# Packed attention and top-1 expert layer: two slots of 256 rows, not four, ahead of the last phase

## The chip, the core and the metric

One core of a Trainium2 chip runs the whole program. The metric is the time of one execution on the device in microseconds (us), the median of several executions; smaller is better. Engines: PE (matrix products), PEld (its weight loads, which overlap PE), DVE (vector), ACT (scalar), POOL (GpSimd, which here mostly issues indirect DMAs), SP (SyncE, which here issues direct DMAs).

## What is computed

```python
# q, k, v: (8 batches, 8 heads, 576 rows, 64); p: (8, 8, 32, 64)
p_packed = softmax(p @ k.T / 8) @ v                  # 32 packed rows per head
x = softmax(q @ p_packed.T / 8) @ p_packed           # laid out as (4608, 512)
logits = x @ w_gate + modality_bias[modality_id]     # 8 experts
e = argmax(logits, 1); gate = softmax(logits)[n, e[n]]
out[n] = gate[n] * (relu(x[n] @ w1[e[n]]) @ w2[e[n]])   # 512 -> 1024 -> 512
```

Each row of the 4608 goes through one expert. Everything is float32; a product is made of three products of the parts of a number, the high part (fp32r) and the residual: high x high, high x residual, residual x high.

With the inputs of the timing, expert 4 gets 2311 rows, expert 5 gets 1406, expert 7 gets 891, the others none. (These counts follow from the reference on the given inputs.)

## The kernel before, in words

Attention runs over batches. Two batches are a pair (there are four pairs), and when a pair's rows of x have been written to a scratch array in device memory (`x_scr`), `routing` finds each row's expert and its place in that expert's list, and puts nine indirect DMAs for the pair into a list `pending`: `scatter` (L488) writes the rows' numbers and gates into the lists (`lst`).

The expert layer works in slots: a slot is a number of rows of one expert that are taken through both products together. There are three phases of slots.

- Phase a (slots 0 and 1): 256 rows each, from pairs 0 and 1 alone, so that they can start while the attention of the later pairs runs.
- Phase b (slots 2 to 5): 256 rows each, from pairs 0 to 2 alone, so that no row of the last pair is waited for. They must be full slots.
- Phase c (the rest): up to 512 rows each, of all pairs; the first of an expert is cut to 384 rows where that avoids an empty fourth tile of 128 (column 6 of the phase's table says which). With these inputs there are seven: 384 and 512 rows of expert 4; 384, 512, 512 of expert 5; 384, 512 of expert 7.

The expert and the rows of each slot stand in tables (`tab_a`, `tab_b`, `tab_c`) that DVE works out at run time, so the slot code loads its values from them and branches on flags. A change of expert means that weights are loaded by SP (L720 for w1, L724 for w2) and split into high part and residual. At the start of phase b and of phase c, the weights of the expert that follows are loaded ahead.

For slot n the steps are these. `go_on(n)` (L1165 and on) issues the last scatter-out of the slot before (L898), empties `pending` as far as slot n+1 needs, calls `turn_of(n+1)` (16 DVE transposes that turn the gathered rows of slot n+1, L802), and puts the loads of slot n+2 into `pending`: one load of list rows into `mt` (L761), then for each tile of 128 rows two indirect gathers `xt<-x_scr,mt` (L768), four in a slot of 256 rows and six in one of 384. `slot(n)` then does the first product (L826 for 256 rows, with four DVE steps L832 that make the residual of the hidden rows; L845 for more rows), prepares the turned rows of slot n+1 (L808, L809) and does the second product (L881). In phases a and b `feed` hands one entry of `pending` to POOL after a step of ACT, so that the entries are spread over the slot.

The numbers of slots are set here, and the end of `pending` here:

```python
    NA = (NP // 2, NP - 1)                                            # (2, 3) pairs
    SA = [max(0, -((E * (P2 - 1) - m * 2 * S) // P2)) for m in NA]    # [2, 6]
...
        if n < SA[1]:
            if n >= SA[0]:
                turn_of(n + 1)
            pre(n + 2)
            if n + 1 == SA[1]:
                held.append(pending.pop())
            if n + 2 >= SA[1]:
                flush()
```

`SA[1]` is the first slot of phase c. `flush()` without an argument hands POOL all that is left in `pending`, the scatters of the last pair among it, because the list rows of a slot of phase c may lie among them.

In the attention part the order of PE, DVE, ACT and SP is written out by hand; POOL, and every engine behind the attention, is ordered by a scheduler when the kernel is built.

Of the kernel before, what the change touches and what calls it, by code (L numbers as in the profile page):

```python
# [23 lines left out]
def packed_attn_moe_kernel(  # L24
# [113 lines left out]

    NA = (NP // 2, NP - 1)
    SA = [max(0, -((E * (P2 - 1) - m * 2 * S) // P2)) for m in NA]  # L140
    NB0 = -(-(N - SA[1] * P2) // P4)
    NB1 = (N - SA[1] * P2 + E * (P4 - 1)) // P4
    NS_ = SA[1] + NB1

# [65 lines left out]
    def need(n):  # L210
        return NA[0] if n < SA[0] else NA[1] if n < SA[1] else NP

# [449 lines left out]
    def two_slots():  # L662


        g = nc.gpsimd
        n = SA[0]
        cnt = sm.tile([P, E], F32, name="cnt_a", bufs=1)
# [130 lines left out]
    def turn(n, ts):  # L798
        g, x = (z[:, ts].rearrange("p t (j n) -> p (t j) n", n=P) for z in (xt_of(n), W["xt"][n >= SA[1]]))
        for z in range(0, P, Q):  # L800
            for w in range(0, P, Q):
                nc.vector.transpose(out=x[w:w + Q, :, z:z + Q], in_=g[z:z + Q, :, w:w + Q])  # L802
# [117 lines left out]
    def xt_of(n):  # L920
        return xts[n % 2 if n < 3 else 1 if n < SA[1] else 2]
# [231 lines left out]
    def last_out(n):  # L1153
        if n >= SA[1]:
            st_out(W, mts[n % 4], 0)

    def go_on(n):
        last_out(n - 1)
        sw(n, 1)
        flush(n + 1)  # L1160
# [8 lines that stand above are left out]
        slot(n)  # L1169
        run(n + 1)  # L1170

    def run(n):
        if n == NS_:
            last_out(n - 1)
        elif n < SA[1] + NB0:
            go_on(n)
# [41 lines left out]
```

## Time and profile before

| | |
|---|---|
| median of 3 runs | 591.72 us (591.26 to 593.12) |
| profiled execution, its own time | 589.05 us |
| its span on the core | 587.5 us |
| PE busy | 549.9 us, 94% |
| DVE busy | 337.6 us, 57% |
| POOL busy | 209.6 us, 36% |
| ACT busy | 208.7 us, 36% |
| mean granted clock of PE | 0.962 of full |

The span runs from the first to the last instruction of the core; the profiled execution's time is 1.55 us longer, and the median of the timed runs is 2.67 us above the profiled one. PE has work for nearly the whole span; the other engines are idle for about half of it or more. All times below count from the start of the span.

### The profile page before, as it was taken

To read this page: it belongs to the slowest core of one execution; us is meant where nothing else is said; L and a number is where in the kernel's file an instruction comes from. 1 tells how busy PE (TensorE), PEld (TensorE's weight loads), DVE (VectorE), ACT (ScalarE), POOL (GpSimd) and SP (SyncE) were. 2 spreads that over 40 slices of the span, in tenths; PEclk is the share of its full clock that TensorE was granted. 3 is DMA by queue.
4 is the path that set the end of the run, shared out by engine and by line. 5 is a ranking of instruction groups with operands and counts; after the bars stand their busy time and mean duration, and the time that the engine had idled before them with its cause. 6 is when DMAs were issued, how large, how long until landed. Compare 5 with 4: busy or idle time off the path is not lost. (4 is left out here: it accounts for less than half of the span.)

```text
span 587.5 us, 11603 instructions
## 1 busy us (share of the span) xinstructions
PE 549.9 (94%) x4408; PEld 461.4 (79%) x4408; DVE 337.6 (57%) x756; ACT 208.7 (36%) x371; POOL 209.6 (36%) x257
## 2 busy tenths in 40 slices
PE   5999997796999999999999999999999999999990
PEld 4777775564788898998999888898888888988880
DVE  1389995758887746453774827349356256285300
ACT  2588884446441212222211324322221242322210
POOL 4003005833355336444443242383503314904120
PEclk9899998967799999999999999999999999999996
DMA  9799996937234742117622124543201202312311
GB/s 290 243 347 370 402 335 221 246 101 244 76 112 114 179 156 70 40 39 162 223 93 65 42 69 107 128 116 122 92 1 56 73 20 58 51 38 62 30 39 39
DMA packets 33685, 77.39 MB, mean 132 GB/s; under 512 B 6768, under 2 KB 6944, under 8 KB 32576
## 3 DMA queue, kind: packets, MB, share of 16 engines
q1 hardware_dynamic: 24224, 54.92, 28.9%
q0 software_dynamic: 8848, 21.28, 13.4%
q8 instruction: 44, 0.72, 0.5%
q14 instruction: 41, 0.34, 0.2%
q10 hardware_dynamic: 528, 0.13, 0.1%
HBM read 57.04 MB, written 19.28 MB: 130 GB/s over the span
## 5 line engine op out<-in xcount | busy, mean ns | idle before, releaser
L768 POOL DMA_INDIRECT xt<-x_scr,mt x86 | 85.6, 995 | 92.1 <-issue 21.8
L802 DVE STREAM_TRANSPOSE rawv<-xt 32x384 f32<-32x384 f32 (+1 forms) x192 | 92.3, 481 | 14.4 <-DMA xt<-x_scr,mt 10.6
L881 PE MATMUL ps_o<-rawq,rawk 128*128 128x512 f32 x272 | 87.2, 391 | 0.0
L898 POOL DMA_INDIRECT out_dram<-ot,mt x37 | 37.3, 1008 | 135.8 <-ACT ot L887 110.5
L845 PE MATMUL ps_h<-x_wide,w1h 128*128 128x512 f32 (+1 forms) x168 | 62.3, 371 | 0.0
L845 PE MATMUL ps_h<-x_wide,w1l 128*128 128x512 f32 (+1 forms) x168 | 61.9, 368 | 0.0
L845 PE MATMUL ps_h<-pT,w1h 128*128 128x512 f32 (+1 forms) x168 | 61.3, 365 | 0.0
L826 PE MATMUL ps_h<-x_hl,w1h 128*128 128x256 f32 x320 | 58.1, 283 | 1.2 <-issue 0.9
L881 PEld LDWEIGHTS ps_o<-rawq,rawk 128*128 128x128 f32 x272 | 51.0, 188 | 10.4
L488 POOL DMA_INDIRECT lst<-meta,dsi x36 | 36.6, 1016 | 52.9 <-ACT st L346 32.5
L826 PEld LDWEIGHTS ps_h<-x_hl,w1h 128*128 128x128 f32 x320 | 49.9, 189 | 2.0 <-issue 1.2
L850 DVE SCALAR_TENSOR_TENSOR rawk<-ps_h,rawk 128x512 fp32r<-128x512 f32 (+1 forms) x28 | 17.4, 633 | 56.9 <-ACT rawk L849 41.2
L826 PE MATMUL ps_h<-x_hl,w1l 128*128 128x256 f32 x160 | 45.4, 285 | 0.0
L887 ACT ACTIVATE ot<-ps_o,mt 128x512 f32<-128x512 f32 x24 | 16.5, 688 | 70.0 <-PE ps_o L881 41.2
L881 PE MATMUL ps_o<-qT,rawk 128*128 128x512 f32 x96 | 37.5, 391 | 0.0
L845 PEld LDWEIGHTS ps_h<-pT,w1h 128*128 128x128 f32 x168 | 31.6, 188 | 4.1
L845 PEld LDWEIGHTS ps_h<-x_wide,w1l 128*128 128x128 f32 x168 | 31.4, 187 | 4.2
L845 PEld LDWEIGHTS ps_h<-x_wide,w1h 128*128 128x128 f32 x168 | 31.6, 188 | 4.0
L300 PE MATMUL ps<-rawv,a1T 64*64 64x128 f32 x576 | 26.9, 299 | 8.3 <-issue 6.5
L849 ACT ACTIVATE rawk<-ps_h 128x512 fp32r<-128x512 f32 (+1 forms) x28 | 15.2, 552 | 49.4 <-PE ps_h L845 47.3
L300 PEld LDWEIGHTS ps<-rawv,a1T 64*64 64x64 f32 x576 | 20.4, 147 | 14.8 <-issue 11.4
L826 PEld LDWEIGHTS ps_h<-x_hl,w1l 128*128 128x128 f32 x160 | 30.2, 189 | 0.1
(266 smaller groups left out, 1138.9 us busy)
## 6 DMA issues: line engine op xcount, KB each, us to landing
rawq<-in_q_dram SPq DMA_DIRECT2D x8, 1152.0 KB
rawv<-in_v_dram SPq DMA_DIRECT2D x8, 1152.0 KB
x_scr<-xs SPq DMA_DIRECT2D x8, 1152.0 KB
raw<-in_moe_w_dram SPq DMA_DIRECT2D x32, 256.0 KB
rawk<-in_k_dram SPq DMA_DIRECT2D x7, 1152.0 KB
kT<-in_moe_w_dram SPq DMA_DIRECT2D x4, 1024.0 KB
qT<-in_moe_w_dram SPq DMA_DIRECT2D x3, 1024.0 KB
xt<-x_scr,mt POOLq DMA_INDIRECT x86
```

Of the source, the lines that this page charges most:

```text
L300: nc.tensor.matmul(pp[u][os_, 0:P], a1T[rs, c, os_], v_t[rs, 2 * pr:2 * pr + 2, TOK[c], :], start=(c == 0), stop=(c == NC - 1), skip_group ...
L488: ins = ins_of(nc.gpsimd.indirect_dma_start(out=lst, out_offset=bass.IndirectOffsetOnAxis(ap=dsi[:, c:c + 1], axis=0), in_=meta[:, i * NC ...
L768: return [free(nc.gpsimd.indirect_dma_start(out=xt[:, t - 2 if t > 1 else 3 - t, u * HW:u * HW + HW], out_offset=None, in_=x_scr[0:NA[ph] ...
L802: nc.vector.transpose(out=x[w:w + Q, :, z:z + Q], in_=g[z:z + Q, :, w:w + Q])
L826: nc.tensor.matmul(ps[:, f], M[a][:, j, (f0 + f) * P:(f0 + f) * P + P], M["x"][b][:, j, 0:P2], start=(n == 0), stop=(n == 3 * KD - 1))
L845: nc.tensor.matmul(ps, M[a][:, j, f * P:f * P + P], M["x"][b][:, j, cs], start=(n == 0), stop=(n == 3 * KD - 1))
L849: ia = nc.scalar.activation(out=hh, in_=ps, func=AF.Relu)
L850: iv = nc.vector.scalar_tensor_tensor(out=hl, in0=ps, scalar=0.0, in1=hh.bitcast(F32), op0=ALU.max, op1=ALU.subtract)
L881: nc.tensor.matmul(op, hid(M, a, j, 1, slice(t * P, t * P + P))[:, 0], M[b][j // 4][:, j % 4], start=(n == 0), stop=(n == 3 * KF - 1))
L887: ia = nc.scalar.activation(out=ot, in_=op, func=AF.Copy, scale=mt.bitcast(F32)[:, row_of(t), 2:3])
L898: nc.gpsimd.indirect_dma_start(out=out, out_offset=bass.IndirectOffsetOnAxis(ap=mt[:, row_of(t), 1:2], axis=0), in_=M["ot"][t == 0], in_of ...
```

## The change

One line limits phase b to two slots more than phase a, so that `SA` is [2, 4] and not [2, 6]:

```diff
@@ -138,6 +138,7 @@
 
     NA = (NP // 2, NP - 1)
     SA = [max(0, -((E * (P2 - 1) - m * 2 * S) // P2)) for m in NA]
+    SA[1] = min(SA[1], SA[0] + 2)
     NB0 = -(-(N - SA[1] * P2) // P4)
     NB1 = (N - SA[1] * P2 + E * (P4 - 1)) // P4
     NS_ = SA[1] + NB1
```

With these inputs phase b then takes slots 2 and 3 (expert 4, as before), and phase c has eight slots: 384, 512, 512 rows of expert 4, and the same five of experts 5 and 7 as before. In all there are 12 slots and not 13: two of 256 rows less, one of 512 rows more. The changes of expert stay two. Lines from 141 on have a number one higher in the changed kernel.

Two places in the order of the built program matter below.

POOL, during slot 1, before: from the first gather of slot 3's rows (into `xt_142`) to the last. `lst<-meta` is a scatter of the last pair, `out_dram<-ot` writes finished rows.

```order
L761 DMA mt_139<-lst 128x2x4 [waits Activation_49]
L768 DMA xt_142<-x_scr,mt_139 128x256 [waits DMASW0_49,Activation_49]
L768 DMA xt_142<-x_scr,mt_139 128x256 [waits Activation_49]
L768 DMA xt_142<-x_scr,mt_139 128x256 [waits DMASW3_49,Activation_49]
L488 DMA lst<-meta,dsi 40960x4 [waits DMASW4_49,DVE_49,Activation_49]
L898 DMA out_dram<-ot,mt_137 4608x512 [waits DMASW5_49,Activation_49]
L768 DMA xt_142<-x_scr,mt_139 128x256 [waits DMASW6_49]
```

The same stretch of POOL after the change:

```order
L769 DMA xt_142<-x_scr,mt_139 128x256 [waits DMASW0_49,Activation_49]
L489 DMA lst<-meta,dsi 40960x4 [waits DVE_49]
L769 DMA xt_142<-x_scr,mt_139 128x256 [waits DMASW3_49,Activation_49]
L489 DMA lst<-meta,dsi 40960x4 [waits DMASW4_49]
L489 DMA lst<-meta,dsi 40960x4 [waits DMASW5_49]
L489 DMA lst<-meta,dsi 40960x4 [waits DMASW6_49]
L489 DMA lst<-meta,dsi 40960x4 [waits DMASW7_49]
L489 DMA lst<-meta,dsi 40960x4
L769 DMA xt_142<-x_scr,mt_139 128x256 [waits DMASW1_49,Activation_49]
L489 DMA lst<-meta,dsi 40960x4 [waits DMASW2_49,Activation_49]
L899 DMA out_dram<-ot,mt_137 4608x512 [waits DMASW3_49,Activation_49]
L769 DMA xt_142<-x_scr,mt_139 128x256 [waits DMASW4_49]
```

The last of the four gathers stood 5 places behind the first, and now stands 11 behind it: seven scatters lie between them where one did, since the emptying of `pending` comes at slot 2 and not at slot 4. The next slot's list load and its six gathers follow this stretch, with two more scatters and one write of finished rows ahead of the gathers.

DVE, in slot 3, before: the turn of slot 4's rows, the four residuals of slot 3's hidden rows (L832), and slot 4's residuals (L809).

```order
L802 STREAM_TRANSPOSE xt_141<-xt_142 32x8x32 x16
L659 TENSOR_LOAD tab_b
L1068 COMPARE_AND_BRANCH
L743 TENSOR_TENSOR qT<-kT,rawq 128x1024 x2
L1056 UNCONDITIONAL_BRANCH
L1068 UNCONDITIONAL_BRANCH
L832 SCALAR_TENSOR_TENSOR rawk<-ps_h_2886,rawk 128x512
L774 UNCONDITIONAL_BRANCH
L832 SCALAR_TENSOR_TENSOR rawk<-ps_h_2887,rawk 128x512
L832 SCALAR_TENSOR_TENSOR rawk<-ps_h_2888,rawk 128x512
L832 SCALAR_TENSOR_TENSOR rawk<-ps_h_2889,rawk 128x512
L809 TENSOR_TENSOR x_hl<-xt_141,x_hl 128x4x128 x2
```

The same place after the change:

```order
L803 STREAM_TRANSPOSE rawv<-xt_2876 32x12x32 x16
L660 TENSOR_LOAD tab_b
L1069 COMPARE_AND_BRANCH
L744 TENSOR_TENSOR qT<-kT,rawq 128x1024 x2
L1057 UNCONDITIONAL_BRANCH
L1069 UNCONDITIONAL_BRANCH
L833 SCALAR_TENSOR_TENSOR rawk<-ps_h_2886,rawk 128x512
L833 SCALAR_TENSOR_TENSOR rawk<-ps_h_2887,rawk 128x512
L833 SCALAR_TENSOR_TENSOR rawk<-ps_h_2888,rawk 128x512
L833 SCALAR_TENSOR_TENSOR rawk<-ps_h_2889,rawk 128x512
```

The turn ahead of slot 3's residuals is now that of a slot with three tiles, 16 transposes of 384 columns and not of 256. Before the change this longer turn stood in slot 5.

## Rows read from the trace of the kernel before

**Rows 1.** The page: the span, and PE's busy time and instructions.

```profile
span 587.5 us, 11603 instructions
...
PE 549.9 (94%) x4408; PEld 461.4 (79%) x4408; DVE 337.6 (57%) x756; ACT 208.7 (36%) x371; POOL 209.6 (36%) x257
```

**Rows 2.** PE's waits, 184.3 to 575: what for, total, times, longest.

```profile
PE ps_h L826 <- issue: 0.9, 2, 0.4
PE ps_h L826 <- ACTq L1068: 0.4, 1, 0.4
```

**Rows 3.** PE's timeline, first matmuls of slots 4, 5, 7, 8.

```profile
254.00 0.41 PE L826 MATMUL ps_h<-x_hl,w1h 128*128 128x256 f32 x2
...
276.45 0.41 PE L826 MATMUL ps_h<-x_hl,w1h 128*128 128x256 f32 x2
...
332.13 0.40 PE L845 MATMUL ps_h<-x_wide,w1h 128*128 128x512 f32 x1
...
375.92 0.35 PE L845 MATMUL ps_h<-x_wide,w1h 128*128 128x384 f32 x1
```

**Rows 4.** POOL's timeline, 199 to 210: start, duration, [idle before it, releaser].

```profile
200.66 0.99 POOL L768 DMA_INDIRECT xt<-x_scr,mt  x1 [8.61 <-DMA mt<-lst]
...
204.45 0.99 POOL L488 DMA_INDIRECT lst<-meta,dsi  x1 [0.30 <-ACT ot L887]
...
207.07 0.99 POOL L768 DMA_INDIRECT xt<-x_scr,mt  x1 [0.30 <-issue]
```

**Rows 5.** POOL's timeline, gathers of slots 4 and 6, and slot 6's list load.

```profile
226.38 0.94 POOL L768 DMA_INDIRECT xt<-x_scr,mt  x1 [0.30 <-issue]
...
260.39 0.79 POOL L761 DMA_DIRECT2D mt<-lst  x1 [0.22 <-issue]
263.58 1.02 POOL L768 DMA_INDIRECT xt<-x_scr,mt  x1 [2.40 <-DMA lst<-meta,dsi]
...
270.02 0.95 POOL L768 DMA_INDIRECT xt<-x_scr,mt  x1 [0.30 <-issue]
```

**Rows 6.** DVE's timeline, turns of slots 3, 4 and 6 and the steps behind.

```profile
214.31 7.17 DVE L802 STREAM_TRANSPOSE xt<-xt 32x256 f32<-32x256 f32 x16 [0.45 <-DVEq L1068]
221.52 1.89 DVE L832 SCALAR_TENSOR_TENSOR rawk<-ps_h,rawk 128x512 fp32r<-128x512 f32 x3
223.32 1.28 DVE L809 TENSOR_TENSOR x_hl<-xt,x_hl 128x512 fp32r<-128x512 f32 x2
229.27 7.18 DVE L802 STREAM_TRANSPOSE xt<-xt 32x256 f32<-32x256 f32 x16 [4.66 <-DMA xt<-x_scr,mt]
236.59 0.69 DVE L832 SCALAR_TENSOR_TENSOR rawk<-ps_h,rawk 128x512 fp32r<-128x512 f32 x1
...
275.82 9.32 DVE L802 STREAM_TRANSPOSE rawv<-xt 32x384 f32<-32x384 f32 x16 [7.57 <-DMA xt<-x_scr,mt]
```

**Rows 7.** PE's timeline, the second products of slot 2 and slot 3.

```profile
220.62 0.40 PE L881 MATMUL ps_o<-rawq,rawk 128*128 128x512 f32 x1
...
224.29 0.62 PE L881 MATMUL ps_o<-rawq,rawk 128*128 128x512 f32 x2
...
243.55 0.62 PE L881 MATMUL ps_o<-rawq,rawk 128*128 128x512 f32 x2
```

**Rows 8.** Slot 3's list load (POOL), w1 loads of phases b and c (SP).

```profile
191.28 0.78 POOL L761 DMA_DIRECT2D mt<-lst  x1
...
184.43 6.70 SPq L720 DMA_DIRECT2D raw<-in_moe_w_dram  x8
...
268.44 7.31 SPq L720 DMA_DIRECT2D raw<-in_moe_w_dram  x8
```

**Rows 9.** Windows: stretch, length, busy PE, PEld, DVE, ACT, POOL, clock, DMA, GB/s.

```profile
133.10:136.50 3.40, 0.50 (x17) 0.25 (x9) 3.23 (x7) 3.40 (x7) 0.00 (x0) 1.00 1.01 355
136.50:143.30 6.80, 5.78 (x66) 4.91 (x69) 6.45 (x16) 5.74 (x9) 3.93 (x4) 0.50 0.70 261
...
180.90:184.30 3.40, 2.80 (x15) 1.92 (x13) 3.02 (x13) 0.69 (x1) 1.56 (x2) 1.00 0.02 1
```

## The prediction

> **What bounds the kernel now.** I first read the page's busy times: PE has 549.9 us of work in a span of 587.5 [rows 1], far more than any other engine. Then PE's waits behind the attention: from 184.3 to 575 it idles 1.3 us in all, in three waits of 0.4 us or so [rows 2]. So in the stretch that the change touches PE alone sets the time, and a microsecond of matmuls there is a microsecond of the end. Third came PE's timeline at the slots' borders, for what a slot costs [rows 3], and last the timelines of POOL and DVE in slots 1 to 6, for how early each slot's rows are ready before PE asks for them [rows 4 to 8]. The reader is to see two things: PE has no slack, and the feeders (list load, gathers, turn) have some, but only a little of it in slot 2.
>
> **PE's work.** The change takes out two slots of 256 rows and adds one of 512 of the same expert. A slot of 256 takes 276.45 − 254.00 = 22.45 us, one of 512 takes 375.92 − 332.13 = 43.79 [rows 3]. The sum is 43.79 − 2 × 22.45 = **−1.1 us**. Nearly all of it is in the first product: 192 matmuls of 256 columns become 96 of 512, and the second product has 96 matmuls of 512 either way. The number of weight changes stays, and so do their loads and splits. Per pair of matmuls the rows give about 1.1 / 96 = 12 ns.
>
> The Trainium skill (TensorE: Matmul & The Clock Gate, "Wait — 56ns, not 53.3ns?") has a fixed cost per matmul at the full clock, about 2.5 ns on top of the columns. By it 96 matmuls less would save an estimated 0.24 us and not 1.1, and the sum below would come out 0.9 us higher. The rows here show the larger saving, since a slot of either kind was measured whole, and I go by them.
>
> **The rows of slot 3, in slot 2.** This is where the change costs something. With two slots in phase b, the emptying of the whole list of pending DMAs comes at slot 2, so seven scatters of the last pair stand among slot 3's gathers on POOL where one did. POOL issues its indirect DMAs one by one: before, the first of slot 3's gathers starts at 200.66 and the last, five places on, at 207.07 [rows 4], so a place costs 6.41 / 5 = 1.28 us. Eleven places on, the last starts at 200.66 + 11 × 1.28 = 214.8, which is 7.7 us later. The nearest landing is that of slot 4's last gather, issued at 226.38, when the turn that waits for it starts at 229.27 [rows 5, 6]: 2.89 us. So slot 3's turn starts at 214.8 + 2.9 = 217.7 and not at 214.31 [rows 6], 3.3 us later. Of the 7.7 us some 4.4 were slack.
>
> What is queued behind it: the turn keeps DVE for 7.2 us, and the residuals of slot 2's hidden rows (second to fourth of L832) stand behind it, then slot 3's residuals (L809). Before, the second residual runs from 221.52 and takes about 0.69 [rows 6]. The second product of slot 2 starts at 220.62, and its 17th matmul, at 224.29, is the first that needs that residual [rows 7] (sixteen that don't are set ahead of it; each takes 0.23 us). Before, it is ready at 222.2, so 2.1 us early. After, it is ready at 221.5 + 3.3 + 0.7 = 225.5, against 224.29: PE waits **1.25 us**. The third and fourth residuals follow 0.6 us apart and are needed later than that, and L809 ends about 3.3 us after the 224.6 of before, 227.9, still ahead of slot 3's first matmul.
>
> The bounds: by the shortest pitch in the rows (0.94 + 0.30 = 1.24 [rows 5]) the turn starts 0.45 us earlier and the wait is 0.8. The longest landing in these rows is that of slot 6's last gather, 270.02 to 275.82, 5.8 us [rows 5, 6], issued beside a weight load [rows 8]; with it the wait would be 4.2. At the time in question no weight load of that size should run, so I take the short landing, but keep 0.8 to 4.2.
>
> **The rows of slot 4, in slot 3.** Slot 4 is now the first wide one. Its list load comes behind the stretch above, at about 216, and its first gather, with two scatters and a write ahead of it, at 221 to 223: behind the list load by 3.2 us at least, as for slot 6 (260.39 to 263.58 [rows 5]). Six gathers take 6.4 us from first to last (263.58 to 270.02), so the last is issued at 227.5 to 229.5 and has landed between 230.4 (by 2.9) and 235.3 (by 5.8). The turn of three tiles takes 9.32 us, not 7.2 [rows 6]. It stands ahead of all four residuals of slot 3, and the first of these is needed by the third matmul of slot 3's second product, at 243.55 [rows 7] plus the 1.25 of the first wait, 244.8. The first residual is ready 0.85 us behind the turn's end, as before (229.27 + 7.18 to 236.59 + 0.69 is 0.83), so at 240.5 to 245.5. I take **0**, since all but the last 0.7 us of this interval is in time; the far end is 0.7.
>
> **What is later.** From slot 4 on, each slot does what slots 6 to 12 did, at the same distances from the turn to the slot: slot 6's turn ends at 275.82 + 9.32 = 285.1 [rows 6], some 14 us before that slot starts, which is at 276.45 + 22.45 = 298.9 [rows 3]. Fewer slots and tables save some steps on DVE, ACT and POOL, which hide under PE and are worth 0.
>
> **Sum.** −1.1 + 1.25 + 0 = about +0.15 us. On the profiled execution's 589.05 that is 589.2; its span is 587.5 and the median of the timed runs is 591.72, 2.67 above it. I add the difference to the median: **591.9 us**. A measurement of this kernel can tell about 0.3%, 1.8 us, from no change, so this forecast is "no change".
>
> **The rivals.**
> - *No wait at all.* The gathers' pitch or the landing come out short enough, or the slack in slot 2 is larger than read. Against it: even the shortest pitch leaves 0.8 us. PE's −1.1 stands alone: 590.6, still within 0.3%.
> - *The wait lowers PE's clock.* In the attention, a PE that had been idle for most of 3.4 us (0.50 busy) at the full clock ran the next 6.8 us at half of it, 1.2 and not 2.4 GHz [rows 9]. Another gap, of 0.6 us in 3.4 (2.80 busy), left the clock full [rows 9]. A wait of 1.25 us is nearer to the second. If the clock falls for 3.4 to 6.8 us, PE loses half of that, 1.7 to 3.4 us: 593.6 to 595.3. This is the one that ends on the slower side, and the wait of 4.2 us among the bounds would resemble the first gap more than the second. It decides as soon as the clock is lost for 3.4 us, since 1.25 − 1.1 + 1.7 = 1.85 is over 0.3%.
> - *Slot 4's rows come late.* The load of w1 ahead of phase c is issued by SP when L809 of its slot is done, which after the change is slot 2's, at about 228, just when slot 4's gathers land. In slot 1 something of the kind is seen: the load of slot 3's list rows, issued at 191.28 behind a w1 load of eight DMAs from 184.43 [rows 8], is waited for until 200.66, with POOL idle for 8.6 us [rows 4]. If slot 4's last gather needed as long (9.4 us), it would land at 237 to 239, the first residual be ready at 247 to 249, and PE wait 2.3 to 4.2 us more: 594.2 to 596. Against it: gathers issued ahead of the load, or just as it starts, need not wait behind it, and slot 6's, issued in the middle of one [rows 8], took 5.8.
> - *The change does nothing*, since the planner would have chosen the same slots: excluded, the built order has them.
>
> On the third: the Trainium skill (DMA: Bandwidth & Descriptors, "SWDGE vs HWDGE vs iDMA") says that each DMA engine goes round between the queues that software and hardware feed. By that a gather beside a weight load would be slowed, not held until the load is through, and the rival would give nothing like 9.4 us. The list load of slot 3 took that long all the same, so the trace does not bear the rule out for a small transfer; I give the rival a chance for it.
>
> **Chances.** A wait of about 1.25 us that gives back the saving: 0.50. No wait or nearly none: 0.15. The clock falls: 0.15. Slot 4's rows late: 0.12. The remaining 0.08 is for what I haven't seen, mostly longer. The first two are within 0.3%, save where the timed median drifts down: faster 0.07, same 0.63, slower 0.30. The range goes from 590.2 (no wait, and 0.4 us for the median's own scatter) to 595.3 (the clock at half for 6.8 us), which leaves out the worse half of the late rows and half of the rest on each side.
>
> **What would show it.** Right: slots 2 and 3 begin at the same times as before, POOL's last gather of slot 3 starts at about 214.8, the turn at 217.7, PE idles 1 to 1.5 us at the 17th matmul of slot 2's second product, and every slot from 4 on runs without a gap. Wrong: no gap there; or a granted clock of 0.5 near 225; or a second gap near 244, with DVE waiting for a DMA ahead of the wide turn; or slots of 512 rows of another length than 43.8 us.

## The result and the profile after

The changed kernel takes 599.88 us (median of 6 runs, 595.14 to 608.76), the kernel before 591.49 (6 runs, 589.59 to 593.12). The ratio is 1.0115, its interval 1.0069 to 1.0162: slower by 1.2%, where "no change" was forecast, and outside the range that was given (590.2 to 595.3). The profiled execution took 599.59. (Two of the changed kernel's runs, 605.65 and 608.76, are left out of the ratio, being over 1.5% above its fastest; the experiments come back to that spread.)

The page, to be read against [rows 1]: the span is 10.5 us longer, and PE's busy time is not.

```profile
span 598.0 us, 11382 instructions
...
PE 547.8 (92%) x4312; PEld 456.0 (76%) x4312; DVE 338.1 (57%) x756; ACT 208.6 (35%) x371; POOL 207.4 (35%) x256
```

So PE idles more, and the chain of waits of PE from 184.3 to 590 (what for, total, times, longest) says for what, against [rows 2]:

```profile
PE ps_h L827 <- issue: 6.5, 8, 1.7
PE ps_o L882 <- issue: 1.1, 2, 0.8
PE ps L463 <- DVE inc L458: 0.3, 1, 0.3
```

The wait that was forecast, of the second product (L882) for DVE, is not there; the one wait for DVE belongs to the routing (L463). "Issue" means that no semaphore, DMA or engine that the trace shows held PE: its next instruction simply came late. PE's timeline shows where, from 208 on, the starts of the first and second products of slots 2 and 3, and of slot 4:

```profile
210.38 0.77 PE L827 MATMUL ps_h<-x_hl,w1h 128*128 128x256 f32 x5
...
212.55 0.28 PE L827 MATMUL ps_h<-x_hl,w1h 128*128 128x256 f32 x1
213.97 0.36 PE L827 MATMUL ps_h<-x_hl,w1h 128*128 128x256 f32 x1 [1.15 <-issue]
216.08 0.37 PE L827 MATMUL ps_h<-x_hl,w1l 128*128 128x256 f32 x1 [1.74 <-issue]
216.82 0.37 PE L827 MATMUL ps_h<-x_hl,w1h 128*128 128x256 f32 x1 [0.37 <-issue]
218.25 0.37 PE L827 MATMUL ps_h<-x_hl,w1h 128*128 128x256 f32 x1 [1.06 <-issue]
218.97 0.58 PE L827 MATMUL ps_h<-x_hl,w1l 128*128 128x256 f32 x1 [0.34 <-issue]
220.39 0.60 PE L827 MATMUL ps_h<-x_hl,w1h 128*128 128x256 f32 x2 [0.85 <-issue]
...
231.10 0.39 PE L882 MATMUL ps_o<-rawq,rawk 128*128 128x512 f32 x1
...
242.02 0.41 PE L827 MATMUL ps_h<-x_hl,w1h 128*128 128x256 f32 x2
...
253.54 0.40 PE L882 MATMUL ps_o<-rawq,rawk 128*128 128x512 f32 x1
...
265.90 0.35 PE L846 MATMUL ps_h<-x_wide,w1h 128*128 128x384 f32 x1
```

From 212.6 to 220.4 the starts lie 0.72 us apart or a multiple of it (216.08 to 216.82, 218.25 to 218.97), where these matmuls otherwise follow each other in 0.12 us. I call this **the stretch**. The first product of slot 2 takes 231.10 − 210.38 = 20.72 us; that of slot 3, undisturbed, 253.54 − 242.02 = 11.52, and before the change that of slot 2 took 11.5 as well (209.09 to 220.62 [rows 7]):

```profile
209.09 0.41 PE L826 MATMUL ps_h<-x_hl,w1h 128*128 128x256 f32 x2
```

What POOL does in the same time, its timeline from 201 (the rows left out are DMAs of the same length, each 0.30 or 0.31 us behind the one before):

```profile
201.76 0.99 POOL L769 DMA_INDIRECT xt<-x_scr,mt  x1 [8.24 <-DMA mt<-lst]
203.05 0.99 POOL L489 DMA_INDIRECT lst<-meta,dsi  x1 [0.30 <-DVE red L520]
...
215.85 0.99 POOL L769 DMA_INDIRECT xt<-x_scr,mt  x1 [0.30 <-issue]
216.83 0.83 POOL L762 DMA_DIRECT2D mt<-lst  x1
217.97 0.99 POOL L489 DMA_INDIRECT lst<-meta,dsi  x1 [0.30 <-issue]
```

The stretch begins 11 us behind the start of the first of these DMAs and ends 2.4 us behind the start of the last. Windows of 3.4 us over it (busy PE, PEld, DVE, ACT, POOL, granted clock, DMA share, GB/s):

```profile
208.20:211.60 3.40, 3.40 (x22) 3.00 (x21) 0.00 (x0) 0.00 (x0) 2.79 (x3) 1.00 0.75 278
211.60:215.00 3.40, 1.59 (x12) 1.39 (x11) 0.00 (x0) 0.00 (x0) 2.49 (x4) 1.00 0.35 28
215.00:218.40 3.40, 0.90 (x3) 0.58 (x2) 0.00 (x0) 0.00 (x0) 2.79 (x4) 0.51 0.45 127
218.40:221.90 3.50, 2.31 (x10) 2.06 (x10) 0.03 (x1) 1.28 (x2) 0.96 (x2) 0.50 0.06 6
221.90:225.30 3.40, 3.40 (x18) 3.40 (x18) 3.30 (x8) 0.00 (x0) 1.56 (x2) 0.50 0.22 78
225.30:228.70 3.40, 3.40 (x30) 3.40 (x30) 3.30 (x8) 0.73 (x2) 2.72 (x3) 1.00 0.25 67
```

Behind the first starved window the granted clock falls to half, 1.2 GHz, and stays there until 225.3, some 5 us longer than the stretch. DVE and ACT do next to nothing in the stretch: they wait for PE, and the DMA engines are far from full.

The span's 10.5 us are then: slot 2 begins 1.29 us later (in the profiles of the result and of `a_again`, `a_second` and `a_third` below its start lies between 207.7 and 210.4, so two executions differ by as much), its first product is 9.2 longer (5.5 of it the waits shown, the rest the half clock and the slow steps between), slot 3's second product 1.43 longer (two more issue waits, 1.1 us, beside a run of seven DMAs), PE's work 1.12 shorter, the remainder −0.3.

The wait that was forecast is covered. DVE's timeline in slot 2:

```profile
221.87 0.69 DVE L833 SCALAR_TENSOR_TENSOR rawk<-ps_h,rawk 128x512 fp32r<-128x512 f32 x1 [14.43 <-ACTq L1069]
222.48 7.19 DVE L803 STREAM_TRANSPOSE xt<-xt 32x256 f32<-32x256 f32 x16
229.70 1.29 DVE L833 SCALAR_TENSOR_TENSOR rawk<-ps_h,rawk 128x512 fp32r<-128x512 f32 x2
```

The turn waits for no DMA: it stands behind a residual that PE's slow product delivers late, and the rest are ready before the second product asks.

### The profile page after: what moved, and what is told of

It reads as the page before. It is cut to its first block, busy times and chain, and to the rows that moved or that the text cites. A ratio compares the mean times of both kernels' runs of the same rounds, so it can differ in the third digit from the quotient of the medians.

```text
span 598.0 us, 11382 instructions
## 1 busy us (share of the span) xinstructions
PE 547.8 (92%) x4312; PEld 456.0 (76%) x4312; DVE 338.1 (57%) x756; ACT 208.6 (35%) x371; POOL 207.4 (35%) x256
## 5 line engine op out<-in xcount | busy, mean ns | idle before, releaser
L803 DVE STREAM_TRANSPOSE rawv<-xt 32x384 f32<-32x384 f32 (+1 forms) x224 | 106.3, 474 | 5.5 <-DVEq L1069 1.2
L882 PE MATMUL ps_o<-rawq,rawk 128*128 128x512 f32 x224 | 72.7, 391 | 0.3 <-issue 0.3
L846 PE MATMUL ps_h<-x_wide,w1h 128*128 128x512 f32 (+1 forms) x192 | 71.8, 374 | 0.0
L846 PE MATMUL ps_h<-x_wide,w1l 128*128 128x512 f32 (+1 forms) x192 | 71.2, 371 | 0.0
L846 PE MATMUL ps_h<-pT,w1h 128*128 128x512 f32 (+1 forms) x192 | 70.6, 368 | 0.0
L882 PEld LDWEIGHTS ps_o<-rawq,rawk 128*128 128x128 f32 x224 | 42.0, 188 | 9.5 <-issue 1.0
L827 PE MATMUL ps_h<-x_hl,w1h 128*128 128x256 f32 x192 | 37.8, 294 | 4.1 <-issue 4.0
L827 PEld LDWEIGHTS ps_h<-x_hl,w1h 128*128 128x128 f32 x192 | 32.2, 201 | 5.1 <-issue 4.6
L301 PEld LDWEIGHTS ps<-rawv,a1T 64*64 64x64 f32 x576 | 20.5, 139 | 19.5 <-issue 15.2
L882 PE MATMUL ps_o<-qT,rawk 128*128 128x512 f32 x88 | 34.3, 390 | 0.8 <-issue 0.8
L882 PE MATMUL ps_t<-rawq,rawk 128*128 128x512 f32 x104 | 34.1, 389 | 0.0
L827 PE MATMUL ps_h<-x_hl,w1l 128*128 128x256 f32 x96 | 28.6, 299 | 2.5 <-issue 2.5
```

The costliest lines, as they stand in the source:

```text
L301: nc.tensor.matmul(pp[u][os_, 0:P], a1T[rs, c, os_], v_t[rs, 2 * pr:2 * pr + 2, TOK[c], :], start=(c == 0), stop=(c == NC - 1), skip_group ...
L827: nc.tensor.matmul(ps[:, f], M[a][:, j, (f0 + f) * P:(f0 + f) * P + P], M["x"][b][:, j, 0:P2], start=(n == 0), stop=(n == 3 * KD - 1))
L846: nc.tensor.matmul(ps, M[a][:, j, f * P:f * P + P], M["x"][b][:, j, cs], start=(n == 0), stop=(n == 3 * KD - 1))
L882: nc.tensor.matmul(op, hid(M, a, j, 1, slice(t * P, t * P + P))[:, 0], M[b][j // 4][:, j % 4], start=(n == 0), stop=(n == 3 * KF - 1))
```

## Experiments

Theories. **Run**: an unbroken run of POOL's indirect DMAs, whatever they move, slows PE's issuing, and the clock falls behind that. **Scatters**: it is these seven scatters, or their targets. **Place**: it is slot 2 (its code, the weights being loaded then), or the two-slot phase as such. **Wait**: as forecast, the last gather's lateness alone, which PE pays for in the second product.

The jobs fell into two groups: in one the kernel before takes 587 to 593 us, in the other 571 to 578. Below they are the *590* and the *575* jobs; each ratio is against the kernel before in the same job. The expectations speak of two kinds of chip. The record has a chip number for each job, and number 6 stands by a job of either group (the kernel before at 575.04 us, and 13 minutes later at 590.12), so that it is the chip which differs is not shown.

### The changed kernel again

`a_again`, `a_second`, `a_third` (590 jobs) and `a_fourth` (575) are the changed kernel as it is.

> The changed kernel once more, to see whether its lost time is always in the same place. In the profile after, slot 2's first product took 20.8 us where 11.5 are normal: PE issued its matmuls 0.72 us apart from 212.6 to 220.4 with nothing named as the reason, and its clock was at half from 215.0 to 225.3. Theory 1 (the run of scatters that stands among slot 3's gathers holds PE's instructions back): the same stretch again, slot 2's first product 16 to 21 us, some 600 us. Rival 2 (such stretches come by chance and anywhere): slot 2's first product is 11.5 us here, or the stretch is in another slot, and the time is near 591 in some executions.

> The changed kernel again, since the last three kernels ran on a chip where the kernel before takes 575 us and not 589 to 592, and where no profile shows PE's slow issuing, not even in the attention. If the slow stretch in slot 2 needs a chip on which PE's issuing is slow in the attention too (L300 with waits that nothing is named for), then: on a chip of 575 us no stretch, slot 2's first product 11.5 us, a wait of 1 to 3 us in its second product, and -1 to +3 us against before; on a chip of 589 us or so again 7 us more. If the stretch comes from the program alone, slot 2's first product is 16 to 21 us on either.

> The changed kernel once more beside these. On a chip with slow issuing as before, 19 to 21 us for slot 2's first product. On one without it: the forecast of the prediction for slot 2, first product 11.5 us, a wait of 1 to 2 us at the 17th matmul of its second product, and a time within 0.3% of before.

> The changed kernel once more, for a chip on which the kernel before takes 574 to 575 us and shows no slow issuing. There: slot 2's first product 11.5 us, a wait of 1 to 2 us at the 17th matmul of its second product, slot 4's rows late by up to 3 us in slot 3's second product, and -1 to +6 us against before as the clock holds or falls. On a chip of 590 us: as in the runs before, 594 to 605.

In the 590 jobs: 596.57 (ratio 1.010, 1.0028 to 1.0172), 604.91 (596.81 to 610.33, no interval), 599.34 (1.0131, 1.0054 to 1.0208). The stretch is in all three profiles, and the first product of slot 2 takes 19.9, 20.0 and 28.7 us. In the last of them, an execution of 605.22, POOL's run did not break: DMAs from 201.51 to 228.87 with 0.3 us between them, where in the first profile it broke behind 217.97. Its stretch lasts from 213 to 231, and PE's issue waits in first products behind the attention (L827) sum to 12.4 us against 6.5. The changed kernel's spread of 594 to 611 us may come from this, whether POOL's run breaks behind that list load; with one profile of the long kind it is not shown.

In the 575 job the kernel takes 579.8 against 575.73, ratio 1.0075 (1.005 to 1.01). There the first product of slot 2 is whole (195.01 to 206.54, 11.53 us) beside the same run of DMAs, and the forecast wait is there. PE:

```profile
214.79 0.73 PE L882 MATMUL ps_o<-rawq,rawk 128*128 128x512 f32 x2 [4.42 <-DVE rawk L833]
```

POOL, the first and the last gather of slot 3:

```profile
189.54 0.99 POOL L769 DMA_INDIRECT xt<-x_scr,mt  x1 [9.96 <-DMA mt<-lst]
...
203.63 0.99 POOL L769 DMA_INDIRECT xt<-x_scr,mt  x1 [0.30 <-issue]
```

DVE:

```profile
206.81 7.20 DVE L803 STREAM_TRANSPOSE xt<-xt 32x256 f32<-32x256 f32 x16 [7.04 <-DMA mt<-lst]
214.04 1.89 DVE L833 SCALAR_TENSOR_TENSOR rawk<-ps_h,rawk 128x512 fp32r<-128x512 f32 x3
```

And the clock, by windows:

```profile
212.20:215.60 3.40, 0.81 (x4) 0.68 (x5) 3.32 (x8) 1.14 (x2) 2.79 (x3) 1.00 0.38 113
215.60:219.00 3.40, 3.40 (x10) 2.63 (x9) 1.53 (x3) 0.00 (x0) 2.26 (x3) 0.51 0.31 88
```

The last gather starts 14.09 us behind the first, as forecast (11 × 1.28 = 14.08), the turn 3.18 us behind it (forecast 2.89), and PE waits at the 17th matmul. The wait is 4.42 and not 1.25, since here the first gather leads the start of slot 2 by 5.47 us (195.01 − 189.54), 2.96 less than in the trace of before (209.09 − 200.66 = 8.43). Slot 1 is 1.06 us shorter than before (23.68 against 24.74), slot 3's list load is issued 0.53 later in it, and POOL's first gather comes 10.75 us behind that issue, not 9.38. 1.25 + 2.96 + 0.29 is 4.5. Then 3.4 us of half clock: the second product takes 17.25 us instead of 10.92, 6.3 more, of which 1.1 come back in the wide slot, so 5.2 by this profile; the timed medians differ by 4.1.

### One part of the change alone

`b_burst` is the kernel before (four slots in phase b) with only the last pair's scatters handed over at slot 2, as the change does (`flush_lists`, whose own lines are left out here, hands POOL every scatter in `pending`):

```diff
+            elif n == SA[0]:
+                flush_lists()
```

`a_lists_first` is the changed kernel with these scatters ahead of slot 3's gathers:

```diff
             pre(n + 2)
+            if n == SA[0] - 1:
+                feed()
+                flush_lists()
```

`a_three` is the changed kernel with three slots in phase b:

```diff
-    SA[1] = min(SA[1], SA[0] + 2)
+    SA[1] = min(SA[1], SA[0] + 3)
```

> The kernel before with its thirteen slots, but with all nine scatters of the last pair handed to POOL at slot 2 and not spread over slots 2 to 5: of the change only the early emptying of the list. Theory 1 (the run of scatters): PE's slow stretch and the half clock appear in slot 2's first product, which takes 16 to 21 us, and the time is 597 to 602. Rival (the stretch belongs to the new sequence of slots, or comes from the wide slot's list load and gathers): no stretch in slot 2, 591 to 593 with at most the 1.25 us wait in slot 2's second product that I forecast.

> The changed kernel, with the nine scatters of the last pair moved ahead of slot 3's gathers, behind slot 3's list load, where POOL stood idle for 8.2 us. If it is the place of the run beside the weight load of w2 and slot 2 (theory 1 in its narrow form), the stretch in slot 2 goes and the time is 589.5 to 591.5, below the kernel before by the 1.1 us of PE's work. If any run of scatters does it, the stretch moves into slot 1 and the time stays at 596 to 602. If the scatters have nothing to do with it, slot 2 is as slow as in the profile after.

> Phase b with three slots (slots 2 to 4), so that the list is emptied one slot later, with three scatters in a row and not five. PE's own work: with five slots of 256 rows the seven wide ones of before stay, so one slot of 256 less than before may be full only by its rows; the matmuls lie between those of before and after. Theory 1: no slow stretch in slot 2, 590 to 593. If the number of slots in phase b matters by itself: between before and after, 594 to 597.

All in 590 jobs. `b_burst`: 601.35, ratio 1.0225 (1.0161 to 1.0289), and again 603.4, 1.0256 (1.0213 to 1.03), as `b_burst_second`; the stretch is in slot 2's first product, 211 to 218, with waits as long as this one:

```profile
213.81 0.37 PE L831 MATMUL ps_h<-x_hl,w1h 128*128 128x256 f32 x1 [1.73 <-issue]
```

So it is not the two-slot phase: the order of POOL's work does it alone, and without the 1.1 us that the change saves. (Its profile has a second loss as well, a wait of 2.3 us in slot 4's second product, whose residuals stand behind two turns on DVE.)

> The kernel before with the early emptying alone, on the same chip as the others of this call. On a chip with slow issuing in the attention: 12 us above before, as in its first run. On one without: no stretch, and a wait of PE in slot 2's second product, 3 to 5 us above before as the last gather of slot 3 starts some 7 us later than in before.

`a_lists_first`: 603.42, 1.0247 (1.0191 to 1.0302). It puts the scatters where POOL waited for slot 3's list load anyway, so that slot 3's rows have nothing new ahead of them, and yet it is slower than the changed kernel: POOL's run lies at 183.92 to 203.07 now, and the stretch has gone with it, to 191 to 207, into the first product of slot 1, which takes 27.4 us where before took 12.9. PE's issue waits behind the attention are 13.5 us in 15. `a_three`: 595.42, 1.0101 (1.0067 to 1.0135). Its run is at 228.25 to 245.99, mostly gathers, with no weight load beside it, and the stretch at 240 to 249.5, in slot 3; its slot 2 has two issue waits of 0.3 us. Place falls: the stretch goes where the run goes.

### Other work for POOL

Each is the kernel before with work added that nothing uses: in slot 2, seven gathers (`b_gathers`, the diff) or in their place seven copies of a tile of rows (`b_work`); among the wide slots, ten gathers (`b_wide`), which stand in the code of slot 8 and which POOL issues during slot 6, not slot 7 as the expectation has it.

```diff
             pre(n + 2)
+            if n == SA[0]:
+                for j in range(7):
+                    nc.gpsimd.indirect_dma_start(
+                        out=xts[2][:, j % 4, j // 4 * HW:j // 4 * HW + HW], out_offset=None, in_=x_scr[0:NA[1] * 4 * S],
+                        in_offset=bass.IndirectOffsetOnAxis(ap=mts[3][:, 2, 0:1], axis=0))
```

> The kernel before with seven gathers added on POOL among slot 3's gathers, in the place of the scatters that the change brings there; they read rows of x that are never used, and the scatters stay spread over slots 2 to 5. Theory 1a (any unbroken run of a dozen indirect DMAs on POOL slows PE's instructions): a slow stretch in slot 2's first product, which takes 16 to 21 us, and the time 5 to 10 us above the kernel before. Theory 1b (it is the scatters, with their 16-byte rows): slot 2's first product 11.5 us, and at most some 7 us of wait in its second product behind the later turn of slot 3's rows.

> The kernel before with seven copies of 128 x 512 on POOL among slot 3's gathers, some 1.3 us each and no DMA; what they write is never used. Rival (it is POOL being busy without a break, whatever it does, or the later turn): a slow stretch in slot 2's first product as with the added gathers. Theory 1a: no slow stretch, slot 2's first product 11.5 us, at most a wait in its second product since the last gather of slot 3 comes later.

> The kernel before with ten gathers added in a row on POOL in slot 7, where PE does matmuls of 512 columns; their rows are never used. Theory 1a as it stands: a slow stretch there too, slot 7 some 4 to 9 us longer than 43.8, and a lower clock. Theory 1c (a run slows PE only where its instructions are many, as in a first product of 256 columns at 0.12 us each): slot 7 stays at 43.8 us and the time within 0.3% of before.

These three came to a 575 job. None has a stretch, the first product of slot 2 is 11.53 us in each. `b_gathers`: 583.72, 1.0145 (1.0114 to 1.0176), a wait of 4.83 us at the 17th matmul of slot 2's second product and 6.8 us of half clock. `b_work`: 580.52, 1.0109 (1.0061 to 1.0157), a wait of 4.11 there and 3.4 us of half clock (its copies took some 0.6 us each and not the 1.3 expected, and POOL stood idle for 4.6 us ahead of them). With `a_fourth` that makes three sizes of the forecast wait, and they follow one rule: the 17th matmul is due 11.53 + 3.67 = 15.2 us behind the start of slot 2 [rows 7], and the residual that it needs is ready some 10.8 us behind the start of slot 3's last gather (2.9 landing, 7.2 turn, 0.7). So PE waits for what that gather is later than 4.4 us into slot 2. It starts 8.94, 8.45 and 8.62 us into it, which gives 4.5, 4.05 and 4.2; measured are 4.83, 4.11 and 4.42. `b_wide`: 567.34, 0.9871 (0.9836 to 0.9907), told below.

> The kernel before with seven unused gathers among slot 3's. On a chip with slow issuing: theory 1a (any run of indirect DMAs) a slow stretch in slot 2's first product, 16 to 21 us; theory 1b (the scatters) 11.5 us. On a chip without: a wait of some 5 us in slot 2's second product, as in its first run.

> The kernel before with ten unused gathers in a row in slot 7. On a chip with slow issuing: theory 1a, slot 7 is 4 to 9 us longer; theory 1c (only where PE's instructions are many), slot 7 is 43.8 us and the time that of before. On a chip without: as in its first run, no wait in slot 7.

In a 590 job the two kernels with gathers have the stretch. `b_gathers_second`: 601.72, 1.0213 (1.0168 to 1.0259), first product of slot 2 21.95 us, run from 200.96 to 217.45. One of its seven waits:

```profile
218.87 0.37 PE L826 MATMUL ps_h<-x_hl,w1l 128*128 128x256 f32 x1 [1.57 <-issue]
```

So the scatters theory falls too: gathers do it. `b_wide_second`: 596.31, 1.0099 (1.0064 to 1.0135). Its run goes from 301.41 to 324.12, and slot 6's first product, which begins at 300.79, on other lines and with 384 columns, takes 29.4 us and not 16.9. Rows of its PE timeline:

```profile
317.17 0.34 PE L845 MATMUL ps_h<-x_wide,w1h 128*128 128x384 f32 x1 [2.00 <-issue]
...
321.40 0.48 PE L845 MATMUL ps_h<-pT,w1h 128*128 128x384 f32 x1 [0.72 <-issue]
```

### How long a run must be

`b_gathers_apart` is `b_gathers` with one addition of 128x1536 on POOL behind the run's seventh DMA; `b_gathers_3` is `b_gathers` with `range(3)`.

```diff
                 for j in range(7):
+                    if j == 3:
+                        src = xts[2][:, 0:1, 0:HW].broadcast_to([P, 6, HW])
+                        nc.gpsimd.tensor_tensor(out=xts[2][:, 1:4].rearrange("p t (u w) -> p (t u) w", u=2), in0=src,
+                                                in1=src, op=ALU.add)
```

> The kernel before with the same seven unused gathers, but with one POOL addition of 128 x 1536 (some 4 us, its result is never used) after the seventh DMA of the run, so that two runs of 7 and 8 stand where one of 14 was. On a chip with slow issuing, if the unbroken length of the run decides: no slow stretch or one under 2 us, slot 2's first product 11.5 to 13.5 us, and in place of it a wait of 4 to 9 us in its second product, since slot 3's last gather comes some 10 us later. If the number of DMAs decides and not the break: 16 to 22 us for the first product, as with the unbroken run.

> The kernel before with three unused gathers in the run and not seven: ten DMAs in a row. In the profiles so far the slow stretch begins 11 to 14 us after the run's first DMA and ends 2 to 4 us after its last. On a chip with slow issuing: a stretch of 1 to 4 us, slot 2's first product 12 to 15 us, no or a short fall of the clock, the time 1 to 5 us above before. If the stretch comes whole from any addition: 20 us and more.

Both in a 590 job. POOL in `b_gathers_apart`, the first and the last DMA of the first run, the pause, and the first DMA of the second run:

```profile
203.91 0.99 POOL L768 DMA_INDIRECT xt<-x_scr,mt  x1 [6.60 <-ACT x_hl L790]
...
211.48 0.94 POOL L768 DMA_INDIRECT xt<-x_scr,mt  x1 [0.30 <-issue]
212.44 2.76 POOL L1169 TENSOR_TENSOR xt<-xt 128x1536 f32<-128x1536 f32 x1
215.37 0.99 POOL L488 DMA_INDIRECT lst<-meta,dsi  x1 [0.17 <-issue]
```

Its chain of waits of PE from 184.3 on:

```profile
PE ps_o L881 <- DVE rawk L832: 3.1, 1, 3.1
PE ps_h L826 <- ACTq L1068: 0.4, 1, 0.4
...
PE ps_o L881 <- issue: 0.2, 1, 0.2
```

The same DMAs, 2.8 us later in the middle: the stretch is gone, slot 2's first product takes 11.53 us, and what comes up in its place is the forecast wait, 3.11 us, with 6.8 us of half clock behind it. The kernel takes 594.23, 1.0084 (1.0055 to 1.0113), against 1.0213 for the unbroken run. `b_gathers_3`, a run of ten from 200.14 to 211.59: a short stretch (two waits, 0.71 and 1.72 us), first product 15.76, 593.71, 1.0066 (1.004 to 1.0093). In slots 2, 3 and 6 the stretch begins 11 to 14 us behind the run's first DMA and ends 2 to 4 us behind its last; in slot 1 (`a_lists_first`) it begins some 7 us behind. Length alone does not decide: a second run of ten in `b_burst` (249.70 to 261.36), and its like in `b_burst_second`, leave no issue wait at all, and a run of seven in slot 3 leaves 1.1 us of them in the result's profile and none in `a_again`.

### The last rival: slot 4's rows

`a_step` is the changed kernel with seven of the scatters (the expectation counts six) and slot 4's loads held back until the first ACT step of slot 2, so that slot 3's gathers stand as before.

```diff
+        if all_at[0] and after is not None:
+            all_at[0] = False
+            while pending:
+                feed(after)
+            return
...
-            if n + 2 >= SA[1]:
+            if n == SA[0]:
+                all_at[0] = True
+            elif n + 2 >= SA[1]:
```

> The changed kernel, with the six remaining scatters of the last pair and slot 4's list load and gathers held back until the first step of ACT in slot 2, so that POOL's order up to there is that of before: a run of seven DMAs, a pause of some 5 us, then about ten. On a chip with slow issuing, if the unbroken run is the cause: slot 2's first product 11.5 to 14 us and not 20. In its place slot 4's rows come late: list load at about 224, last gather at 235, turn of three tiles from 238 to 247, first residual of slot 3 ready at 248 where 243.6 is wanted, so a wait of 4 to 5 us at the third matmul of slot 3's second product and, as behind the wait of 3.1 us in the run with the pause, a half clock for some 6.8 us (3.4 us). Together 590 - 1.1 + 4.6 + 3.4 = 597, or 593.5 if the clock holds. If the change is slow for another reason: slot 2's first product stays at 20 us and the time above 600.

In a 575 job: 592.01, 1.0307 (1.0261 to 1.0352), the worst of all, so it says nothing of the stretch. Slot 2 is clean (11.53 and 10.92 us). But slot 4's list load is issued at 214.57 only, and its gathers run from 221.43 to 227.78, the first beside the end of the w1 load, the last beside two loads of w2 that SP issues at 227.45 and 228.10; the turn, and PE:

```profile
234.97 9.31 DVE L810 STREAM_TRANSPOSE rawv<-xt 32x384 f32<-32x384 f32 x16 [23.96 <-DMA xt<-x_scr,mt]
```

```profile
245.06 1.22 PE L889 MATMUL ps_o<-rawq,rawk 128*128 128x512 f32 x2 [15.23 <-DVE rawk L840]
```

I had expected 4 to 5 us there. So the third rival's mechanism, slot 4's rows late, is real, with a price of 15 us once slot 4's list load comes 10 us later than in the changed kernel of the other 575 job (214.57 against 204.61 in `a_fourth`). The last gather landed 7.19 us behind its issue (227.78 to 234.97), the one before it in 2.79. In the trace's DMA packets POOL's queue moves nothing from 229.0 to 232.5, while the queue of the w2 loads moves packets throughout, and then packets beside theirs; the gather lands behind the first load (233.56) and ahead of the last packet of the second (236.78). By the Trainium skill (DMA: Bandwidth & Descriptors, "SWDGE vs HWDGE vs iDMA") each DMA engine goes round between the queues that software and hardware feed. That agrees with the second part of the 7.19 us and not with the first, so this trace decides neither for the rule nor against it.

## Why the prediction was wrong, step by step

- *PE's work, −1.1*: right. A slot of 512 takes 342.90 − 299.12 = 43.78 us after the change (forecast 43.79), slot 3, where nothing disturbs it, 22.46 in `a_again`. The saving is in every profile of the changed kernel, 1.12 us. The smaller saving of 0.24, by the fixed cost per matmul that the Trainium skill gives (TensorE: Matmul & The Clock Gate, "Wait — 56ns, not 53.3ns?"), isn't borne out.
- *POOL's pitch, the last gather 11 places on*: right to 0.01 us in both groups of jobs (201.76 to 215.85, 189.54 to 203.63).
- *The wait at the 17th matmul, 1.25 us*: right in place and mechanism, wrong in size in the 575 job (4.42): how far the gathers lead slot 2 was read from a single execution, and it changes with the length of slot 1 and with the list load ahead of them, 9.0 to 10.8 us from its issue to the first gather. In the result the wait is hidden under the stretch.
- *Slot 4's rows, 0*: right (no wait for slot 4's rows in any profile of the changed kernel); `a_step` shows how near the edge is.
- **The step that failed** is the one that priced the seven scatters by their pitch alone: POOL's longer run was taken to cost nothing but a later turn, and PE's first product of slot 2 to be untouched ("slots 2 and 3 begin at the same times as before"). In the result and in the other 590 jobs the unbroken run itself slows PE's issuing, and that and the clock behind it cost 8 to 17 us in slot 2's first product.
- *The rival of the clock* had half of it: the granted clock was at half near 225, from 215.0 to 225.3, but behind starved issuing in the first product, not behind the wait. The waits of 3.11, 4.11, 4.42 and 4.83 us in `b_gathers_apart`, `b_work`, `a_fourth` and `b_gathers` did each bring 6.8, 3.4, 3.4 and 6.8 us at half clock, as that rival said. Its chance of 0.15 looks too small for the 575 jobs, where the wait was about its far bound of 4.2.

The trace of before held the sign, in a stretch that I read for its clock alone. The chain of waits of PE in the attention, 0 to 185, begins with

```profile
PE ps L300 <- issue: 6.5, 14, 1.0
```

and five of these waits lie beside an unbroken run of the first pairs' scatters. POOL's timeline from 89 to 97, and PE's from 90 to 99:

```profile
90.21 1.12 POOL L488 DMA_INDIRECT lst<-meta,dsi  x1 [32.49 <-ACT st L346]
...
95.60 0.97 POOL L488 DMA_INDIRECT lst<-meta,dsi  x1 [0.42 <-issue]
```

```profile
94.55 0.46 PE L300 MATMUL ps<-rawv,a1T 64*64 64x128 f32 x4 [0.29 <-issue]
95.30 0.27 PE L300 MATMUL ps<-rawv,a1T 64*64 64x128 f32 x1 [0.29 <-issue]
96.06 0.43 PE L300 MATMUL ps<-rawv,a1T 64*64 64x128 f32 x3 [0.49 <-issue]
96.79 0.27 PE L300 MATMUL ps<-rawv,a1T 64*64 64x128 f32 x1 [0.29 <-issue]
```

Starts 0.75 us apart, as in the stretch. The profiles of the 575 jobs show at most 1.1 us of such waits in the whole attention. That these waits have the same cause as the stretch was not tried: no run moved the first pairs' scatters.

## What to carry to other kernels

An "issue" wait of the engine that sets the time is a cost to be explained before work is moved: look at what the other engines do beside it. Indirect DMAs on POOL are not free for PE merely because POOL has time: a run of them without a pause cost up to 17 us here, and a pause of 2.8 us in its middle took the stretch away. And a lead read from one execution is not a constant: the gathers' lead over slot 2 was 3 us shorter in another job, and the wait 3 us longer.

## What the runs showed of the hardware that was not expected

- **PE issues slowly beside an unbroken run of POOL's indirect DMAs**, 0.72 us or a multiple of it from one matmul to the next instead of 0.12 to 0.17, in the 590 jobs and not in the 575 ones. Shown: the run causes it (it goes where the run goes, with scatters or gathers, in slots of all three phases and with matmuls of two widths, and is gone with a pause). Not shown: by what path POOL's DMAs reach PE's issuing, what a run must have beside its length, and why one group of jobs has it and the other not. From 239 to 250 in `a_three`, beside its stretch, POOL's own queue is the only one whose packets the trace shows (403 of them), so there neither a weight load nor a load of instructions is the path. That POOL's being busy with copies doesn't do it was tried in a 575 job alone, where gathers don't do it either, so that is open as well.
- **The two groups of jobs** differ by 2.5% for the kernel before (medians 589 to 591 and 574 to 576). Nearly all of it lies ahead of slot 2, which begins at 207.7 to 210.9 us in the profiles of the 590 jobs (222.1 in `a_lists_first`, whose stretch is ahead of it) and at 194.1 to 198.6 in those of the 575 jobs. In `before` the issue waits up to there sum to 8.4 us, and PE runs 27 us at half clock between 99 and 154; in `b_wide` and `a_fourth` there are none of these waits (over 0.25 us), and 10 and 14 us at half clock. By an estimate from these numbers (8.4 us, and half of the 13 to 17 us) slow issuing and the clock behind it are about the whole of the 14 us (209.09 against 195.01).
- **The end of the program** takes 13.3 to 14.0 us behind PE's last matmul in before, in after and in most runs, but 6.0 in `b_wide` and `b_wide_second`, which add ten gathers some 270 us earlier, and 8.8 in `a_three`, which adds none. In the 575 job, with no stretch to pay, this made `b_wide` 1.3% faster than before, the only kernel here that beats both; in the 590 job the 12.6 us of its stretch took more than that back. What in the end of the program got shorter is not settled, and no kernel that has the short end and a broken run was tried.
